# Splitting the float64 weights with a sloped ReLU, with guard, shift and query scaling on VectorE

## The chip, the cores and the metric

The kernel runs on one NeuronCore of a Trainium2 chip. The metric is the device time of one execution in microseconds (us), as the median of several runs. Engine names are those of the profile: PE is TensorE (PEld its weight loads), DVE is VectorE, ACT is ScalarE, POOL is GpSimd, SP is SyncE, which issues most DMAs.

## The reference

Attention with a threshold, then a SwiGLU feed-forward block. The batch is 8, with 8 heads, 576 positions and 64 values a head; the block has 4608 tokens, width 512 and inner width 1536.

```python
scores = scale * np.matmul(q, k.transpose(0, 1, 3, 2))      # scale = 1/8
thresh = np.max(scores, axis=-1, keepdims=True) - tau
scores = np.where(scores >= thresh, scores, -1000000000.0)
attn = np.exp(scores - np.max(scores, axis=-1, keepdims=True))
attn = attn / (np.sum(attn, axis=-1, keepdims=True) + 1e-09)
x = (attn @ v)            # -> (8*576, 512)
...
g = x @ w_gate
silu = g * (1.0 / (1.0 + np.exp(-g)))
return (silu * (x @ w_val)) @ w_out
```

q, k and v are float32. The three weight matrices come as float64.

## The kernel before

**Stages.** The first batch is worked through in two passes, ahead of everything else. Pass one (stage 1, to about 51 us) goes over four pairs of heads with two score tiles of 128 queries each, eight tiles T0 to T7. Pass two (stage 2, to about 129 us) goes over the pairs again with the three tiles that are left of each, the third a half tile (L468); plain products of the feed-forward block (L571) are filled in between. Stage 3 (to about 269 us) brings the first of the later batches, with jobs that a planner puts in order by costs and due times written in the code, and the output products of the first batch. After that a steady state runs to the end, in which PE alternates scores, weighted sums and the products of the feed-forward block. In stages 1 and 2 the order on each engine is the order in which the code issues, tile by tile: the loop over `segs[:2 * NP]` calls `scores`, and between its `next(go)` steps the other work.

**A tile.** PE makes the scores of two heads into two PSUM tiles (L462). DVE takes the maximum of each (L479, two reductions), ACT the exponential (L482, twice) and the threshold (L484), DVE the masks with their sums (L487, twice, which free the PSUM tiles), then the total and its reciprocal (L489, L490). The next tile needs the same PSUM. PE transposes the masked tile (L517, L520), multiplies it by v (L545, L548, L550), ACT copies (L557) and POOL multiplies the two heads' parts (L558). At the end of a tile DVE transposes k and q of the next pair (L682, L685) or the rest of q (L770). The factor 1/8 of the scores is applied to q: by DVE for the first pair (L684), for the others by POOL (L395, queued by `scales`).

**The weights.** [...]

- `split_weights`: ACT reads the upper word as float32 and writes its scaled absolute value (L322); ACT turns the lower word into a small number (L323).
- `clamp` (L315): bounds the absolute value. It runs on POOL in stages 1 and 2, and on DVE for two pieces of stage 3.
- `shift_weights`: DVE shifts the result left by three bits (L342). The exponent field comes out as that of float32.
- `join_weights`: DVE puts the sign back, which it takes from the upper word in the place of the load (L348, between L479 and L487 of the next tile). Then the place is free for the next load.
- `add_lower`: POOL adds the lower word's contribution to the bits (L358).

In stage 3 the last pieces go the same way as jobs: L890 and L893 on ACT, L315, L900 and L902 on DVE, L904 on POOL. In stage 2 three tiles handle two pieces at once (`double`).

**Score order (L462).** Head 0 first, in two halves of 288 keys, then head 1 in pieces of 64, 224 and 288 keys.

**Halves.** The sigmoid is made of a tanh, and several factors of one half are put into ACT's scale operand (the tanh's argument, the copies of the sums) or into a DVE operation (L1083, L1209).

## Time and profile before

| | us |
|---|---|
| median of 3 runs | 1366.19 (1366.06 to 1366.28) |
| profiled execution, its own time | 1368.65 |
| span of the profile of that execution | 1366.5 |
| mean granted clock of PE | 0.996 |

The profile comes from one execution. Its own time is 2.15 us above the span, for what lies around the program, and 2.46 us above the median of the unprofiled runs. A row of the timeline has the start, the duration, the engine, the line and operation, the tile written and the tiles read (partitions x elements), a count, and in brackets the idle time of the engine ahead of it with what ended that. Rows in sequence may overlap by some 0.08 us, since an engine starts the next instruction before the last has left it.

### The profile page before, as it was taken

What the parts mean: (1) busy time and instruction counts of PE and PEld (TensorE: products, weight loads), DVE (VectorE), ACT (ScalarE), POOL (GpSimd) and SP (SyncE); (2) the same over time, 40 slices, a digit from 0 to 9 for tenths busy, and PEclk for the clock granted to TensorE, in tenths of its full rate; (3) what the DMA queues carried; (4) which work ended last, traced back from release to release, by engine and by line L of the source; (5) the groups of instructions that cost most, each with busy time, mean ns of one, the idle gap of its engine ahead of it and who ended that gap; (6) DMA issues with size and microseconds to landing.
All of it is one profiled execution on the core that took longest, in us unless ns stands there. A gap on an engine that the chain in (4) does not pass through costs nothing.

```text
span 1366.5 us, 39110 instructions
## 1 busy us (share of the span) xinstructions
PE 1346.2 (99%) x15598; PEld 1124.6 (82%) x15598; DVE 1094.1 (80%) x2860; ACT 857.4 (63%) x2190; POOL 710.8 (52%) x676
## 2 busy tenths in 40 slices
PE   8899999999999999999999999999999999999998
PEld 6687877777788788877888788888887788999888
DVE  6889898888887878887878777887888776797786
ACT  6788765677765777677767677677767674330330
POOL 2777698754655669434963387337843592000000
PEclk9999999999999999999999999999999999999999
DMA  7753323466426431654255514643255404424411
GB/s 173 192 197 102 72 60 114 129 177 179 114 48 167 149 81 46 183 144 113 45 170 137 152 19 138 158 139 68 74 156 145 110 27 158 149 77 142 160 54 32
DMA packets 208293, 162.31 MB, mean 119 GB/s; under 512 B 166128, under 2 KB 180464, under 8 KB 202736
## 3 DMA queue, kind: packets, MB, share of 16 engines
q1 hardware_dynamic: 203920, 158.86, 41.3%
q8 instruction: 123, 2.02, 0.6%
q10 hardware_dynamic: 4192, 0.95, 0.3%
q14 instruction: 58, 0.48, 0.1%
HBM read 138.28 MB, written 21.50 MB: 117 GB/s over the span
## 4 chain that ended last, share of the span: by engine, by line
PE 91%; DVE 4%; DMA 2%; SPq 1%; ACT 1%; issue 1%; ACTq 0%; DVEq 0%
PE pb L1012 17%; PE pa L1012 12%; PE px L1501 12%; PE sc L1761 10%; PE pe L1012 9%; PE xa L1895 9%; PE po L1294 5%; PE py L1510 5%; PE sc L1179 1%; PE sc L462 1%; PE pe L1179 1%; PE pg L1225 1%; PE pv L571 1%; PE sc L1012 1%; PE pg L571 1%
## 5 line engine op out<-in xcount | busy, mean ns | idle before, releaser
L1837 ACT ACTIVATE pall<-sc,nm 128x288 f32<-128x288 f32 x504 | 234.7, 501 | 79.1 <-DVE pall L1839 43.9
L1839 DVE SCALAR_TENSOR_TENSOR pall<-sc,th,pall 128x288 f32<-128x288 f32 x504 | 243.6, 512 | 38.5 <-ACT pall L1837 22.0
L1012 PE MATMUL pb<-xall,big 128*128 128x256 f32 x1104 | 262.0, 380 | 0.0
L1012 PEld LDWEIGHTS pb<-xall,big 128*128 128x128 f32 x1104 | 207.5, 190 | 29.6 <-issue 1.6
L1874 DVE STREAM_TRANSPOSE pall<-pall 128x576 f32<-128x576 f32 x252 | 187.9, 763 | 28.7 <-POOL pall L1869 15.2
L1872 ACT ACTIVATE pall<-pall,ri 128x288 f32<-128x288 f32 x416 | 190.5, 526 | 22.7 <-DVE ri L1860 21.9
L1012 PE MATMUL pa<-xall,big 128*128 128x256 f32 x752 | 178.9, 381 | 0.3 <-ACT sc L1019 0.3
L1012 PEld LDWEIGHTS pa<-xall,big 128*128 128x128 f32 x752 | 140.7, 190 | 20.9 <-issue 2.5
L863 POOL TENSOR_TENSOR hall<-hall,tmp 128x512 f32<-128x512 f32 x80 | 102.7, 1283 | 104.8 <-DVE hall L1071 64.5
L1761 PE MATMUL sc<-kT,qT 64*32 64x288 f32 (+1 forms) x5376 | 146.9, 345 | 1.5 <-issue 1.2
L1796 DVE TENSOR_REDUCE mx<-sc 128x2 f32<-128x576 f32 x168 | 118.3, 746 | 35.4 <-PE sc L1761 34.5
L1869 POOL TENSOR_SCALAR pall<-pall,ri 128x288 f32<-128x288 f32 x88 | 88.2, 1010 | 105.1 <-DVE ri L1860 75.9
L1761 PEld LDWEIGHTS sc<-kT,qT 64*32 64x32 f32 x5376 | 98.0, 106 | 53.3 <-issue 12.8
L1012 PE MATMUL pe<-xall,big 128*128 128x256 f32 x576 | 138.4, 383 | 0.0
L1895 PE MATMUL xa<-pall,vall 64*32 64x288 f32 x4032 | 129.4, 404 | 3.0 <-PE px L1501 2.7
L1012 PEld LDWEIGHTS pe<-xall,big 128*128 128x128 f32 x576 | 107.6, 190 | 18.7 <-issue 4.5
L1895 PEld LDWEIGHTS xa<-pall,vall 64*32 64x32 f32 x4032 | 83.4, 107 | 41.7 <-issue 5.0
L863 POOL TENSOR_TENSOR tmp<-tmp 128x512 f32<-128x512 f32 x36 | 45.9, 1276 | 83.5 <-ACT tmp L1093 83.5
L1854 ACT COPY sums<-sums 32x6 f32<-32x6 f32 x336 | 66.6, 198 | 28.0 <-DVE pall L1839 23.8
L1070 ACT ACTIVATE vall<-tmp 128x512 f32<-128x512 f32 x96 | 60.0, 627 | 34.5 <-DVE tmp L1083 27.2
L1510 PE MATMUL py<-wo,hall 128*128 128x256 f32 x336 | 74.8, 379 | 0.0
L863 POOL TENSOR_TENSOR hall<-hall 128x384 f32<-128x384 f32 (+2 forms) x67 | 67.6, 1023 | 8.9 <-PE px L1501 8.2
(268 smaller groups left out, 2493.7 us busy)
## 6 DMA issues: line engine op xcount, KB each, us to landing
big<-sums_hbm SPq DMA_DIRECT2D x42, 1024.0 KB, 5.2
big<-sums_hbm SPq DMA_DIRECT2D x48, 768.0 KB, 4.8
vall<-in_v_dram SPq DMA_DIRECT2D x112, 144.0 KB, 3.0
out_dram<-big SPq DMA_DIRECT2D x32, 256.0 KB, 2.9
qT<-in_q_dram SPq DMA_DIRECT2D x112, 72.0 KB, 4.8
kT<-in_k_dram SPq DMA_DIRECT2D x112, 72.0 KB, 3.1
wo<-in_moe_w_gate_dram SPq DMA_DIRECT2D x16, 384.0 KB, 4.2
wo<-in_moe_w_val_dram SPq DMA_DIRECT2D x16, 384.0 KB, 5.1
```

Of the source, the lines that this page charges most:

```text
L863: return lambda: nc.gpsimd.tensor_tensor(out=out, in0=a, in1=b, op=op)
L1012: nc.tensor.matmul(ps[:, i], w[:, k_, i * P:(i + 1) * P], x[:, k_, :], start=first and i == k_ == 0, stop=True, skip_group_check=True)
L1501: nc.tensor.matmul(ps, a[:, f, :], ws[n][:, f, :], start=bank_ not in begun, stop=True, skip_group_check=True)
L1510: nc.tensor.matmul(ps(), a[:, f, i * P:(i + 1) * P], operands[o][:, f, :], start=first and f == 0, stop=True, skip_group_check=True)
L1761: nc.tensor.matmul(to[g * G:(g + 1) * G], qT[hs, col:col + G], kT[hs, c * SH + lo:c * SH + hi], start=True, stop=True)
L1796: rs.append(job("DVE", 0.72 if w > 1 else 0.42, lambda h=h: nc.vector.tensor_reduce(out=mx[:, n0 + h:n1 + h + 1:max(2, n1 - n0), 0], in_=s ...
L1837: ej = job("ACT", 0.44, lambda x=x, n=n: nc.scalar.activation(ps[x], scs[x], AF.Exp, bias=nm[:, n:n + 1]), ej, rank=top, on=on[x])
L1839: masks[x] = job("DVE", 0.48, lambda x=x, n=n: nc.vector.scalar_tensor_tensor(out=ps[x], in0=scs[x], scalar=th[:, n:n + 1], in1=ps[x], op0 ...
L1869: scaled.append(job("POOL", 1.02, lambda x=x, n=n: nc.gpsimd.tensor_scalar(out=x, in0=x, scalar1=ri[:, n:n + 1], scalar2=None, op0=ALU.mul ...
L1872: scaled.append(job("ACT", 0.46, lambda x=x, n=n: nc.scalar.activation(x, x, AF.Copy, scale=ri[:, n:n + 1]), rj, rank=rank))
L1874: seg["turned"].append(job("DVE", 0.72, lambda both=both: nc.vector.transpose(out=both, in_=both), *scaled, rank=rank))
L1895: nc.tensor.matmul(holds[a].ap()[x * G:(x + 1) * G, 0:SH].rearrange("d (i q) -> d i q", q=G), vr[rs, h, j, ds], p[rs, h, :, j, :], start=( ...
```

## The change

- The upper word is read through a sloped ReLU (`Prelu`), so that the sign stays and the xor (L348, L902) is gone; `join_weights`, `clamp_split` and `add_lower` go with it.
- The clamp works on the upper 16 bits of each result as an integer, on DVE, directly ahead of the shift. Both stand at the end of a tile, where the shift stood. POOL's add is issued right behind the shift.
- The lower word becomes an integer by ACT's conversion on output. A place is free for the next load when ACT has read the lower word.
- q of the first batch is scaled by DVE directly ahead of each transpose (128x256 with the pair's k and q, 128x320 for the rest of q).
- The five score products of a tile alternate between the heads: head 0's first half, head 1's 64 and 224, head 0's second half, head 1's second.
- Most factors of one half leave ACT's scale operand and are collected in the copies of the attention's sums (0.5 in the first batch, 0.25 later).

By the order of the instructions on each engine: POOL loses 22 clamps and 7 scalings; DVE loses 24 xors and gains 22 clamps on top of the two that it had and 7 scalings on top of the one; PE has the five products of stage 1's and 2's tiles in another order; SP issues two pieces of weights of stage 1 ahead of a v load and, in stage 3, the last piece ahead of a k and q load. ACT's instructions keep their shapes.

```diff
@@ -309,66 +311,46 @@
     def words(place, dst, w):
         return places[place].bitcast(U32).rearrange("p (m n w) -> p m n w", m=dst.shape[1], w=2)[:, :, :, w]
 
-    early_slots, clamped, unclamped, shifted, unsummed = [True], [], deque(), [], []
 
     def clamp(eng, x):
-        eng.tensor_scalar(out=x, in0=x, scalar1=1.875 * 2.0 ** -80, scalar2=2.0 ** -111, op0=ALU.min, op1=ALU.max)
+        top = x.bitcast(I16).rearrange("p m (n w) -> p m n w", w=2)[:, :, :, 1]
+        eng.tensor_scalar(out=top, in0=top, scalar1=float((32 << 7) - 2 ** 15), scalar2=float((31 << 7) + (7 << 4)), op0=ALU.max, op1=ALU.min)
+
+    def upper(dst, place):
+        nc.scalar.activation(dst, words(place, dst, 1).bitcast(F32), AF.Prelu, scale=2.0 ** -112, alpha=2.0 ** 32)
+
+    def lower(lo, dst, place):
+        nc.scalar.activation(lo.bitcast(I32), words(place, dst, 0), AF.Copy, bias=2.0 ** 23, scale=2.0 ** -29)
 
     def split_weights():
         if fetched:
             dst, place = fetched.popleft()
             lo = los[0].rearrange("p (m n) -> p m n", m=dst.shape[1])
             los.rotate(1)
-            nc.scalar.activation(dst, words(place, dst, 1).bitcast(F32), AF.Abs, scale=2.0 ** -96)
-            nc.scalar.activation(lo, words(place, dst, 0), AF.Identity, bias=minus2, scale=-2.0 ** -51)
-            unclamped.append(dst)
-            if early_slots[0]:
-                clamp_split()
+            upper(dst, place)
+            lower(lo, dst, place)
+            used.discard(place)
             split.append((dst, place, lo))
 
-    def clamp_split():
-        while unclamped:
-            dst = unclamped.popleft()
-            clamp(nc.gpsimd, dst)
-            clamped.append(dst)
+    def shift(dst):
+        ub = dst.bitcast(U32)
+        clamp(nc.vector, dst)
+        nc.vector.tensor_scalar(out=ub, in0=ub, scalar1=3, scalar2=None, op0=ALU.logical_shift_left)
 
     def shift_weights(n=1):
 
-        steps = [split.popleft() for _ in range(min(n, len(split)))]
-        if any(up is x for up, place, lo in steps for x in unclamped):
-            clamp_split()
-        for up, place, lo in steps:
+        for up, place, lo in [split.popleft() for _ in range(min(n, len(split)))]:
             ub = up.bitcast(U32)
-            nc.vector.tensor_scalar(out=ub, in0=ub, scalar1=3, scalar2=None, op0=ALU.logical_shift_left)
-        shifted.extend(steps)
-
-    def join_weights():
-        for up, place, lo in shifted:
-            ub = up.bitcast(U32)
-            nc.vector.scalar_tensor_tensor(out=ub, in0=words(place, up, 1), scalar=0x80000000, in1=ub,
-                                           op0=ALU.bitwise_and, op1=ALU.bitwise_xor)
-            used.discard(place)
-        unsummed.extend(shifted)
-        shifted.clear()
-        add_lower(min(1, len(unsummed)))
-
-    def add_lower(n):
-        for up, place, lo in unsummed[:n]:
-            ub = up.bitcast(U32)
+            shift(up)
             nc.gpsimd.tensor_tensor(out=ub, in0=ub, in1=lo.bitcast(U32), op=ALU.add)
             joined.append(up)
-        del unsummed[:n]
 
     def need(n):
-        if len(joined) < n:
-            join_weights()
-            add_lower(2)
         while len(joined) < n:
             fetch_weights(2)
             if not split:
                 split_weights()
             shift_weights()
-            join_weights()
             split_weights()
 
     raw_places = {0: h1all[:, 0:2 * S], 1: extra[:, 0:2 * S], 2: extra[:, 2 * S:4 * S], 3: h1all[:, 2 * S:4 * S]}
@@ -405,17 +387,12 @@
                 nc.vector.tensor_scalar(out=cap, in0=tau_s, scalar1=0.0, scalar2=2e38, op0=ALU.is_ge, op1=ALU.mult)
                 nc.vector.tensor_scalar(out=cap, in0=cap, scalar1=-1e38, scalar2=None, op0=ALU.add)
                 nc.vector.scalar_tensor_tensor(out=cut, in0=tau_s, scalar=-1.0, in1=cap, op0=ALU.mult, op1=ALU.min)
-            elif i == 1:
-                scale(raws[0][:, 0:QA])
-            else:
-                scales.append(lambda: scale(raws[0][:, 0:QA]))
 
             own = h1all[:, 4 * S:5 * S - QA] if i == 0 else raws[0][:, QA:S]
             raws.append(own)
 
             def load_rest():
                 load("q", slice(QA // G, NJ), [nc.sync] * 2, own.rearrange("p (j d) -> p j d", d=G))
-                scales.append(lambda: scale(own))
 
             more_loads.append(load_rest)
         else:
@@ -444,9 +421,6 @@
 
     heads = [slice(h * D, (h + 1) * D) for h in range(2)]
 
-    def turned(t):
-        return t < NT
-
     def statistics(*names):
         return [stp.tile([P, 2 * MU, 2] if x == "mx" else [P, 2 * MU], F32, name=x) for x in names]
 
@@ -455,12 +429,10 @@
         q0 = t * P - seg["q0"]
         if t < NT:
             pss = [next_sc() for _ in range(2)]
-            for h, hs in enumerate(heads):
-                cut_ = D if turned(t) and h == 1 else 0
-                for n, lo, to in [(0, 0, D), (0, D, SH), (1, 0, SH)] if cut_ else [(0, 0, SH), (1, 0, SH)]:
-                    at_ = (n * SH + lo - cut_) % S
-                    nc.tensor.matmul(pss[h][:, n, lo:to], qT[hs, q0:q0 + P], kT[hs, at_:at_ + to - lo],
-                                     start=True, stop=True)
+            for h, n, lo, to in ((0, 0, 0, SH), (1, 0, 0, D), (1, 0, D, SH), (0, 1, 0, SH), (1, 1, 0, SH)):
+                hs, at_ = heads[h], (n * SH + lo - h * D) % S
+                nc.tensor.matmul(pss[h][:, n, lo:to], qT[hs, q0:q0 + P], kT[hs, at_:at_ + to - lo],
+                                 start=True, stop=True)
         else:
             pss = [next_sc()]
             for n, h in ((0, 0), (1, 1), (1, 0), (0, 1)):
...
@@ -554,7 +526,7 @@
         rbufs.rotate(1)
 
         def weigh():
-            nc.scalar.copy(both, xa[:, 0:2 * n])
+            nc.scalar.activation(both, xa[:, 0:2 * n], AF.Copy, scale=0.5)
             nc.gpsimd.tensor_tensor(out=to, in0=both[:, 0:n], in1=both[:, n:2 * n], op=ALU.mult)
 
         copy(xa, weigh)
...
@@ -669,6 +641,9 @@
         if i < NPAIR and i not in raws and i not in kept:
             raws[i] = load_qk(i)
 
+    def scale_q(x):
+        nc.vector.tensor_scalar(out=x, in0=x, scalar1=scl, scalar2=None, op0=ALU.mult)
+
     def prepare(seg):
         i = seg["i"]
         if i in kept:
@@ -680,8 +655,7 @@
             qT = qkp.tile([P, S], F32, name="qT")
             kT, rest_ = kTs[i], rests[i]
             nc.vector.transpose(out=kT, in_=kr)
-            if i == 0:
-                nc.vector.tensor_scalar(out=qr[:, 0:QA], in0=qr[:, 0:QA], scalar1=scl, scalar2=None, op0=ALU.mult)
+            scale_q(qr[:, 0:QA])
             nc.vector.transpose(out=qT[:, 0:QA], in_=qr[:, 0:QA])
             later.append((rest_, raws[i][2]))
             kept[i] = {"kT": kT, "qT": rest_, "q0": QA}
@@ -714,13 +688,11 @@
     more_loads.popleft()()
     last = iter(())
     for n, seg in enumerate(segs[:2 * NP]):
-        early_slots[0] = n < NP
         if n >= NP:
             seg["v"] = segs[seg["i"]]["v"]
         for x, t in enumerate(seg["tiles"]):
             go = scores(seg, t)
             next(go)
-            join_weights()
             if not n and not x:
                 run_idle(6)
             next(last, None)
@@ -748,8 +720,6 @@
                 split_weights()
                 fetch_weights(2)
             next(go)
-            clamp_split()
-            add_lower(1)
             double = t == NT and NP <= n < NP + 3
             if more and not double:
                 shift_weights()
@@ -759,7 +729,6 @@
             if double:
                 shift_weights(2)
                 split_weights()
-                clamp_split()
                 fetch_weights(2)
             gates()
             last = go
@@ -767,17 +736,14 @@
                 later.rotate(1)
             if later and (n == NP or n == NP - 1 and x == 0):
                 to, fr = later.popleft()
+                scale_q(fr)
                 nc.vector.transpose(out=to, in_=fr)
             if x == 0 and 0 < n < NP - 1:
                 load_v(segs[n + 1])
                 more_loads.popleft()()
-            if n == 0 and x == 1 or n == 1:
-                scales.popleft()()
-            elif n == NP - 2 and x == 1:
+            if n == NP - 2 and x == 1:
                 more_loads.popleft()()
-                scales.popleft()()
             elif n == NP - 1:
-                scales.popleft()()
                 fetch_qk(NP)
             elif n == NP and x == 1:
                 scales.popleft()()
@@ -785,7 +751,6 @@
                 prepare(segs[n + 1])
 
     fill(left[0])
-    join_weights()
     fetch_weights()
     gates()
 
@@ -887,23 +852,17 @@
                 before = joins[-3] if len(joins) > 2 else None
 
                 def up_part(dst=dst, place=place):
-                    nc.scalar.activation(dst, words(place, dst, 1).bitcast(F32), AF.Abs, scale=2.0 ** -96)
+                    upper(dst, place)
 
                 def lo_part(dst=dst, place=place, lo=lo):
-                    nc.scalar.activation(lo, words(place, dst, 0), AF.Identity, bias=minus2, scale=-2.0 ** -51)
+                    lower(lo, dst, place)
 
                 j = job("ACT", 0.93, up_part, j if srcs else landed, done.get(place), under, rank=2)
-                j = job("ACT", 1.03, lo_part, j, before, rank=2)
+                j = done[place] = job("ACT", 1.03, lo_part, j, before, rank=2)
             ub = dst.bitcast(U32)
-            if not any(dst is x for x in clamped):
-                j = job("DVE", 0.6, lambda dst=dst: clamp(nc.vector, dst), j, rank=2)
-            j = job("DVE", 0.6, lambda ub=ub: nc.vector.tensor_scalar(
-                out=ub, in0=ub, scalar1=3, scalar2=None, op0=ALU.logical_shift_left), j, rank=2)
-            j = job("DVE", 0.96, lambda ub=ub, dst=dst, place=place: nc.vector.scalar_tensor_tensor(
-                out=ub, in0=words(place, dst, 1), scalar=0x80000000, in1=ub, op0=ALU.bitwise_and, op1=ALU.bitwise_xor), j, rank=2)
+            j = job("DVE", 1.2, lambda dst=dst: shift(dst), j, rank=2)
             j = job("POOL", 1.85, lambda ub=ub, lo=lo: nc.gpsimd.tensor_tensor(out=ub, in0=ub, in1=lo.bitcast(U32), op=ALU.add), j, rank=2)
             joins.append(j)
-            done[place] = j
         return joins
 
     stores, summed_g, parts = {}, {}, []
...
@@ -1080,8 +1039,7 @@
         def p3(self):
             m = self.mul(self.e, self.w[5], xs[2], False, self.s5, *self.w_deps[5], *ready_x[self.c][4])
             u = self.u1_buf
-            g1 = job("DVE", 0.7, lambda: nc.vector.scalar_tensor_tensor(out=u.ap, in0=self.e.rows(), scalar=0.5, in1=u.ap, op0=ALU.mult,
-                                                                        op1=ALU.add), m, self.u1, rank=0)
+            g1 = job("DVE", 0.7, lambda: nc.vector.tensor_tensor(out=u.ap, in0=self.e.rows(), in1=u.ap, op=ALU.add), m, self.u1, rank=0)
             self.e.read_by(g1)
             self.e.done(True)
             self.finish(0, u, g1, self.a, self.m2)
...
@@ -1903,8 +1861,9 @@
         lo, at_last = 0, 2 * NT * G
         for a in range(R):
             def copy(a=a):
-                nc.scalar.copy(xk[:, a], holds[a].ap()[:, lo:lo + 2 * NT * G].rearrange("p (t i q) -> p t i q", t=2, q=G))
-                nc.scalar.copy(xl[:, a], holds[a].ap()[:, at_last:at_last + G])
+                nc.scalar.activation(xk[:, a], holds[a].ap()[:, lo:lo + 2 * NT * G].rearrange("p (t i q) -> p t i q", t=2, q=G),
+                                     AF.Copy, scale=0.25)
+                nc.scalar.activation(xl[:, a], holds[a].ap()[:, at_last:at_last + G], AF.Copy, scale=0.25)
             js.append(job("ACT", 0.65, copy, m, last_store[0] if cc == 0 else None, rank=0))
             holds[a].read_by(js[-1])
             holds[a].done(False)
```

## The prediction, made before the changed kernel was run

> **What bounds the kernel now.** I read the page first, then the windows by stage, the waits of PE, and the timelines of DVE, POOL and PE around the longest wait.
>
> ```profile
> PE 1346.2 (99%) x15598; PEld 1124.6 (82%) x15598; DVE 1094.1 (80%) x2860; ACT 857.4 (63%) x2190; POOL 710.8 (52%) x676
> ```
>
> PE is busy for 99% of the span, so a change pays only where PE waits or runs slowly. The windows show where that is.
>
> ```profile
> core 0: us, PE busy (x) PEld busy (x) DVE busy (x) ACT busy (x) POOL busy (x), PEclk, DMA share, GB/s
> 0.00:51.25 51.25, 42.44 (x299) 33.77 (x300) 38.59 (x91) 33.18 (x63) 23.82 (x28) 0.90 0.82 191
> 51.25:128.93 77.68, 76.15 (x609) 60.01 (x610) 66.32 (x127) 63.46 (x120) 56.49 (x50) 1.00 0.49 152
> 150.00:182.00 32.00, 31.57 (x435) 26.33 (x433) 31.36 (x85) 22.47 (x64) 25.79 (x24) 1.00 0.19 39
> 269.00:1366.00 1097.00, 1088.76 (x12814) 921.00 (x12798) 863.87 (x2289) 666.79 (x1752) 520.21 (x498) 1.00 0.41 116
> ```
>
> Stage 1 (to 51.25, eight score tiles T0 to T7) leaves PE idle for 8.8 us, at a mean granted clock of 0.90. Stage 2 leaves 1.5. From 150 to 182 DVE is busy 98% of the time, PE idle 0.4. Nothing that matters changes after 269.
>
> ```profile
> PE sc L462 <- DVE pall L487: 6.3, 5, 3.7
> ```
>
> A score tile cannot start before the masks (L487) of the tile before have freed its PSUM: five waits, 6.3 us, the longest 3.7. That one is the stall below, first on DVE, then on POOL, then on PE.
>
> ```profile
> 32.19 0.17 DVE L490 RECIPROCAL ri<-tot 128x2 f32<-128x2 f32 x1
> 34.79 0.88 DVE L342 TENSOR_SCALAR big<-big 128x768 uint32<-128x768 uint32 x1 [2.43 <-POOL big L315]
> 36.61 1.38 DVE L479 TENSOR_REDUCE nm<-sc 128x1 f32<-128x576 f32 x2
> 37.92 1.05 DVE L348 SCALAR_TENSOR_TENSOR big<-wo,big 128x768 uint32<-128x768 uint32 x1
> 40.76 1.10 DVE L342 TENSOR_SCALAR big<-big 128x768 uint32<-128x768 uint32 x1
> ```
>
> ```profile
> 30.83 0.93 POOL L395 TENSOR_SCALAR hall<-hall,scl 128x256 f32<-128x256 f32 x1 [5.97 <-DMA hall<-in_q_dram]
> 31.72 1.81 POOL L358 TENSOR_TENSOR big<-big,extra 128x768 uint32<-128x768 uint32 x1
> 33.92 0.83 POOL L315 TENSOR_SCALAR big<-big 128x768 f32<-128x768 f32 x1
> 39.63 1.81 POOL L358 TENSOR_TENSOR big<-big 128x768 uint32<-128x768 uint32 x1
> ```
>
> ```profile
> 39.76 3.24 PE L462 MATMUL sc<-pall,qT 64*128 64x288 f32 x10 [3.74 <-DVE pall L487]
> ```
>
> POOL's queue stands behind a q scaling that waits for its load, so the clamp is late, the shift waits 2.43 behind the clamp, and T6 starts after 3.74 of idle PE. The granted clock then is 0.50 from 38.96 to 45.79: T6 takes 3.24, where tiles at full clock take 1.36 to 2.09.
>
> Also to be seen: the shift at 40.76 takes 1.10 and ends 0.42 after POOL's add of 39.63. Alone it takes 0.54 (row at 46.44). A second case:
>
> ```profile
> 81.39 1.82 POOL L358 TENSOR_TENSOR big<-big,extra 128x768 uint32<-128x768 uint32 x1
> 81.99 2.04 DVE L348 SCALAR_TENSOR_TENSOR big<-wo,big 128x768 uint32<-128x768 uint32 x1
> ```
>
> The xor, 0.95 alone, takes 2.04 and ends 0.82 after the add. DVE's shift or xor and POOL's add do not overlap: the later one waits.
>
> **Stage 1, part by part.** Removed: the clamps L315 and the scalings L395 of the first batch from POOL (0.83 to 1.25 each here), the xors from DVE. Added on DVE: a 16-bit clamp before each shift, a q scaling before each q transpose. No row shows that clamp. Below it lie float clamp and shift of the same 128 x 768 (0.55, 0.54), above it the xor (0.95); I take 0.54, the row that also reads one source. The scaling is 0.31 for 128x256 (L684), about 0.35 for 128x320. ACT's two passes stay two of 128 x 768 (L322 0.93, L323 1.05). The sloped form is in no row; between those two I price it at 0, since ACT is idle by 0.49 and 0.50 around its early pieces, and a tenth more would hide there.
>
> The xor lay between L479 and L487, mostly beside ACT's exp: L479 to L487 takes 2.21 with it (23.67 to 25.88) and 1.76 without it (two tiles before 17). So a tile loses 0.45 and gains a clamp of 0.54 that nothing hides.
>
> - T1: one scaling, +0.34.
> - End of T2 (from 21.7): clamp 0.54; POOL's product L558 is due and goes first (0.46); shift 0.54, k transpose 0.7. POOL's add starts 0.08 behind the shift and runs 1.82, so the scaling, due 0.7 behind the shift, waits some 1.2 for it; then 0.31 and the q transpose 0.4. L479 of T3 starts near 25.8 against 23.67, +2.1; without the xor T4's scores are 1.65 late.
> - T3 to T5: +1.7. At the end of T4 the 2.43 of waiting is gone, but product, clamp and add come in turn again: from 33.6, 0.54 + 0.46 + 0.54 + 0.08 + 1.82 + 0.31 + 0.4 give L479 near 37.8, against 36.61. T6's scores come at 40.5, +0.8.
> - The half clock costs 2.8 (T6 3.24 for 1.36, its sums 1.92 for 1.04). PE's idle time before T6 would be 2.8 instead of 3.74, so I let half stay: -1.4.
>
> Stage 1 ends near 50.6 instead of 51.25: **-0.6**. Bounds: +0.8 if all of the half clock stays; -2.0 if all goes; -3.8 if the scalings also do not wait for the adds (2.5 of stall and 2.8 of clock, less three scalings and six times 0.09).
>
> The Trainium skill, page "SBUF — State Buffer", section "Who interferes with whom", calls the port pair of VectorE and GpSimd an exclusive lock for a whole instruction. The rows above agree (0.42 and 0.82 past the add's end). By a shared port instead of a lock the sum would take the -3.8.
>
> Score order: in the trace head 1's first product starts 13 ns after head 0's first, though two of head 0 stand ahead of it. Where head 1 waits for the second mask it starts 0.74 later in either order, and head 0's second half then stands behind it. I price it at 0, bounds 0 to +0.15 a waiting tile. The Trainium skill, "TensorE: Matmul & The Clock Gate", Part 2, says that matmuls stay in program order; this trace differs by those 13 ns.
>
> Weight places now come free behind ACT's lower read, so SP issues two pieces ahead of a v load: those pieces land some 4 us earlier (40.76 before), v of the next pair about 40.7, still before T6's sums. If v came later than those sums, PE would wait for the difference; I take 0.
>
> **Stage 2.** Three places (73.2, 91.9, 110.6) handle two pieces in a row: clamp, shift, clamp, shift. POOL's add of the first piece is pending when the second clamp ends, and the second shift follows with 0.03 between. I take it that the pending add goes first. At 73.2: 0.54 + 0.62 + 0.08 + 0.54 + 1.82 + 0.55, then scaling and transpose 0.74; less what overlaps, L479 is near 77.6 instead of 74.80. Without the two xors (2.12) L487 is 1.2 later than at 78.15, and the scores at 79.01 with it. The two others have no scaling: +0.5 and +0.6. What follows regains nothing, since PE is full there (98%). Sum **+2.3**. If DVE keeps the port: L487 comes earlier, and what can be gained is 0.37 of idle PE at 116.31 and 0.73 a tile where head 1 waits (2.09 against 1.36), some -1.7 in all.
>
> **Stage 3.** Six pieces lose xors of 0.95 to 1.36 on DVE and a float clamp; two clamps are there before and shifts stay. PE idle from 128.9 to 214 is 1.25, of which 0.58 waits for ACT. I take the rest: **-0.7**, bounds 0 and -1.25.
>
> **Steady state.** Copy and activation forms cost ACT 580 to 596 ns alike, the half-scaled add 0.69 as the plain one: 0.
>
> **Sum:** -0.6 + 2.3 - 0.7 = +1.0. The profiled execution took 1368.65 (span 1366.5 and 2.15 around it), so 1369.65 for it; the median is 2.46 lower, which gives **1367.2**.
>
> **Rivals.**
> - *Slower: the 16-bit clamp costs what the xor did, 0.95.* For it: its step of two and its type occur nowhere in the trace. Against it: one-source rows of the same size take 0.54. Six tile ends of stage 1 and three first clamps of stage 2 get 0.41 longer (the second clamps lie beside the add), +3.7, in all +4.7: **1370.9**. From 0.75 on it decides.
> - *DVE keeps the port at the double pieces.* -0.6 - 1.7 - 0.7 = -3.0: **1363.2**. For it: DVE issues its next instruction before the last has ended (starts overlap by 0.08 in the rows). Against it: the add asks first.
> - *No wait behind adds at all, for scaling or second shift.* -3.8 - 1.7 - 0.7 = -6.2: **1360.0**. For it: a POOL scaling beside DVE slows it little (0.55 to 0.56 beside L1869). Against it: the two pairs of rows above.
> - *Alternation pays:* if products really start in order, head 1 would start some 0.6 earlier in each of the eight tiles of stage 1, which gives about -5, less what the masks still hold back: **1362**. Against it: 13 ns. (The rule beside it is that of Part 2 of the TensorE page of the Trainium skill.)
>
> **Chances.** Forecast 0.37, slow clamp 0.25, DVE keeps the port 0.19, no waits 0.13, alternation 0.06. The bound of 0.2% (2.73 us, about what a measurement of this kernel can tell from no change) lies at 1363.46 and 1368.92. Faster: 0.01 + 0.17 + 0.13 + 0.05 = 0.36. Slower: 0.06 of the forecast (half clock stays) and 0.24 of the slow clamp, 0.30. Within: 0.34. The forecast's own range is 1365 to 1369.5; with the other cases it is 1360.5 to 1371.2, which leaves out about half of "no waits" and a tenth above.
>
> **What would show it.** Right: the wait of 2.43 gone; scaling rows of about 1.5 behind the k transpose at the ends of T2 and T4; T3's L479 near 25.8; scores of T6 near 40.5 after 2 to 3 of idle PE; second shifts of 2.4 at the three doubles; clamp rows of 0.54; from 269 on the same distance to the end. Wrong: scalings of 0.31 there, clamp rows of 0.95, T6 at full clock, PE waiting for v.

## The result, and the profile after

The changed kernel takes 1374.44 us (median of 7 runs, 1370.40 to 1375.52) against 1366.53 for the kernel before (7 runs). The ratio is 1.0044, with a 95% interval of 1.0030 to 1.0058: slower by some 6 us (the two medians lie 7.9 apart). The profiled execution took 1374.44, its span is 1372.5, 6.0 more than the span before. One execution, of e6_before_filled in the table of the experiments, took 2314.55 us at a mean clock of 0.556 and is left out of its ratio.

The page of the changed kernel, first the engines:

```profile
PE 1350.1 (98%) x15598; PEld 1123.8 (82%) x15598; DVE 1088.4 (79%) x2865; ACT 854.4 (62%) x2190; POOL 678.0 (49%) x647
```

DVE and POOL both have less to do than before (1088 for 1094, 678 for 711), and the kernel is slower. The sum of the work is not the reason. The windows by stage, with the same bounds as before:

```profile
core 0: us, PE busy (x) PEld busy (x) DVE busy (x) ACT busy (x) POOL busy (x), PEclk, DMA share, GB/s
0.00:51.25 51.25, 43.84 (x288) 33.24 (x288) 39.63 (x92) 31.12 (x59) 12.61 (x17) 0.87 0.87 208
51.25:128.93 77.68, 73.35 (x575) 56.80 (x571) 57.52 (x124) 59.02 (x115) 36.34 (x30) 0.98 0.47 141
...
150.00:182.00 32.00, 31.46 (x435) 26.29 (x434) 28.48 (x77) 23.41 (x68) 29.45 (x29) 1.00 0.16 29
...
269.00:1372.00 1103.00, 1094.67 (x12959) 923.32 (x12957) 868.81 (x2308) 669.62 (x1763) 520.45 (x498) 1.00 0.41 116
```

The mean granted clock of the first window fell from 0.90 to 0.87, and of the second from 1.00 to 0.98. DVE is busy 1.0 us more than before in the first and 8.8 us less in the second. The last window is 6 longer and holds 6 more of PE's work only because the same work comes 6 later; from stage 3's first scores to the end it takes as long as before (worked out below). PE's waits:

```profile
PE sc L434 <- DVE pall L459: 8.5, 7, 2.5
```

Seven waits of score tiles for the masks, 8.5 us, where there were five of 6.3. The longest is 2.5 instead of 3.7. Line numbers have moved: L434 is L462 of before, L459 is L487, L451 is L479, L338 the shift, L317 the new clamp, L645 the q scaling, L345 POOL's add. On DVE, the ends of T2 and T4 and the second double (a double handles two pieces of 128 x 768 weights in a row):

```profile
23.49 0.77 DVE L338 TENSOR_SCALAR big<-big 128x768 uint32<-128x768 uint32 x1
24.18 0.77 DVE L657 STREAM_TRANSPOSE pall<-extra 128x576 f32<-128x576 f32 x1
24.88 1.43 DVE L645 TENSOR_SCALAR extra<-extra,scl 128x256 f32<-128x256 f32 x1
...
26.72 1.38 DVE L451 TENSOR_REDUCE nm<-sc 128x1 f32<-128x576 f32 x2
...
35.12 0.60 DVE L317 TENSOR_SCALAR big<-big 128x768 int16<-128x768 int16 x1
35.76 0.56 DVE L338 TENSOR_SCALAR big<-big 128x768 uint32<-128x768 uint32 x1
...
36.93 1.44 DVE L645 TENSOR_SCALAR hall<-hall,scl 128x256 f32<-128x256 f32 x1
...
38.78 1.38 DVE L451 TENSOR_REDUCE nm<-sc 128x1 f32<-128x576 f32 x2
...
96.22 0.63 DVE L317 TENSOR_SCALAR big<-big 128x768 int16<-128x768 int16 x1
96.88 2.01 DVE L338 TENSOR_SCALAR big<-big 128x768 uint32<-128x768 uint32 x1
```

POOL's adds at the same places:

```profile
24.34 1.82 POOL L345 TENSOR_TENSOR big<-big,extra 128x768 uint32<-128x768 uint32 x1 [0.49 <-DVE big L338]
...
36.41 1.82 POOL L345 TENSOR_TENSOR big<-big 128x768 uint32<-128x768 uint32 x1 [1.75 <-DVE big L338]
...
96.38 2.08 POOL L345 TENSOR_TENSOR big<-big,extra 128x768 uint32<-128x768 uint32 x1 [3.64 <-DVE big L338]
99.03 1.80 POOL L345 TENSOR_TENSOR big<-big 128x768 uint32<-128x768 uint32 x1 [0.56 <-DVE big L338]
```

The add starts at 24.34 and runs to 26.16; the scaling of 24.88 ends at 26.31, 0.15 behind it, and takes 1.43 instead of 0.31. The same happens at 36.41 and 36.93. At 96.38 the add starts beside the second clamp and takes 2.08 instead of 1.82; the second shift of 96.88 ends 0.43 behind the add and takes 2.01. Read as in the prediction, the pending add goes as soon as the clamp has ended, and the shift waits for it. The clamp by itself takes 0.60.

The score tiles that wait, and the stretches of half clock:

```profile
16.59 3.24 PE L434 MATMUL sc<-pall,qT 64*128 64x288 f32 x10 [1.91 <-DVE pall L459]
...
24.47 1.36 PE L434 MATMUL sc<-pall,qT 64*128 64x288 f32 x10
...
41.41 3.23 PE L434 MATMUL sc<-pall,qT 64*128 64x288 f32 x10 [2.54 <-DVE pall L459]
...
82.20 2.09 PE L434 MATMUL sc<-pall 64*128 64x288 f32 x10 [1.38 <-DVE pall L459]
...
120.73 2.09 PE L434 MATMUL sc<-pall 64*128 64x288 f32 x10 [1.01 <-DVE pall L459]
```

```profile
core 0: us, PE busy (x), PEclk, DMA share, GB/s
17.30:24.13 6.83, 6.83 (x38) 0.50 0.93 260
41.20:48.03 6.83, 6.62 (x35) 0.50 0.97 282
123.10:126.50 3.40, 3.40 (x28) 0.50 0.02 5
```

The third column of the last fence is the granted clock. The half clock lasts 6.83 us from 17.3, 6.83 from 41.2 and 3.41 from 123.1, 17.1 us in all. Before it was 3.41 from 18.5 and 6.83 from 39.0, 10.2 in all.

Where the 6.0 come in, by the starts of the score tiles against those of before:

| place | late by | what came in |
|---|---|---|
| T2 (16.59) | 0.48 | the scaling ahead of T1, and 0.09 at the start |
| T3 (24.47) | 2.07 | T2 to T3 7.88 instead of 6.29: two windows of half clock instead of one |
| T4 (29.35) | 2.60 | the scaling behind the add |
| T6 (41.41) | 1.65 | the wait of 2.43 is gone, the second scaling waits |
| end of stage 1 (53.05) | 1.80 | T6 at half clock as before |
| behind the doubles | 3.19, 3.79, 4.42 | the second shifts: 1.38, 0.60, 0.63 |
| last half tile (129.03) | 6.02 | 8.30 instead of 6.70 from tile to tile: the half clock at 123 |
| end | 6.0 | stage 3 adds 0.6, and 0.6 is regained behind it |

So 2.6 come from the doubles, 3.5 from half clock (1.59 from T2 to T3; 0.29 from T6 to T7, which takes 7.43 instead of 7.14; 1.60 at 123), and the queues of stage 1 by themselves give -0.1. This is read from two executions, one of each kernel; e4 below bears on it.

### The profile page after: what moved, and what is told of

Its sections match the earlier page's. It is cut to its first block, busy times and chain, and to the rows that moved or that the text cites. A ratio compares the mean times of both kernels' runs of the same rounds, so it can differ in the third digit from the quotient of the medians.

```text
span 1372.5 us, 39057 instructions
## 1 busy us (share of the span) xinstructions
PE 1350.1 (98%) x15598; PEld 1123.8 (82%) x15598; DVE 1088.4 (79%) x2865; ACT 854.4 (62%) x2190; POOL 678.0 (49%) x647
## 4 chain that ended last, share of the span: by engine, by line
PE 91%; DVE 5%; ACT 2%; issue 1%; DMA 1%; POOL 0%; SPq 0%; DVEq 0%; ACTq 0%; POOLq 0%
PE pb L971 17%; PE pa L971 12%; PE px L1459 12%; PE sc L1719 10%; PE pe L971 9%; PE xa L1853 9%; PE py L1468 5%; PE po L1252 4%; PE sc L434 1%; PE pg L1183 1%; PE sc L1137 1%; PE pv L1183 1%; PE pe L1137 1%; PE pv L543 1%; PE sc L971 1%
## 5 line engine op out<-in xcount | busy, mean ns | idle before, releaser
L1797 DVE SCALAR_TENSOR_TENSOR pall<-sc,th,pall 128x288 f32<-128x288 f32 x504 | 243.8, 513 | 39.9 <-ACT pall L1795 23.6
```

Of the source, the lines that this page charges most:

```text
L1797: masks[x] = job("DVE", 0.48, lambda x=x, n=n: nc.vector.scalar_tensor_tensor(out=ps[x], in0=scs[x], scalar=th[:, n:n + 1], in1=ps[x], op0 ...
```

## The experiments

Two theories. "Lock": DVE's scaling and second shift wait for POOL's add, since the shift now releases the add directly ahead of them. "Clock": the idle time that this makes on PE brings more stretches of half clock, and those are the larger part. Its opposite in the expectations, "chain", says that only the waits for VectorE count. The rivals are in the expectations. Each kernel was timed against the kernel before on the same chip.

| kernel | median, us | ratio to before | 95% interval |
|---|---|---|---|
| the changed kernel | 1374.44 | 1.0044 | 1.0030 to 1.0058 |
| e1_fill | 1375.26 | 1.0052 | 1.0039 to 1.0065 |
| e2_scale_first | 1369.63 | 1.0014 | 1.0005 to 1.0023 |
| e3_doubles | 1369.65 | 1.0011 | 1.0001 to 1.0022 |
| e4_order | 1372.54 | 1.0038 | 1.0025 to 1.0052 |
| e5_fill_transposes | 1373.73 | 1.0044 | 1.0032 to 1.0057 |
| e6_before_filled | 1369.46 | 1.0013 | 1.0004 to 1.0022 |
| e7_before_scale_vector | 1368.54 | 1.0007 | 0.9998 to 1.0016 |
| e8_after_scale_gpsimd | 1368.95 | 1.0003 | 0.9994 to 1.0012 |
| c1_both | 1363.45 | 0.9973 | 0.9963 to 0.9984 |
| c2_both_filled | 1364.76 | 0.9981 | 0.9972 to 0.9990 |
| c3_both_order | 1362.80 | 0.9968 | 0.9956 to 0.9981 |
| c4_pair1_gpsimd | 1363.51 | 0.9968 | 0.9956 to 0.9980 |

### e2: the scaling ahead of the shift

```diff
-            scale_q(qr[:, 0:QA])
+            if i == 0:
+                scale_q(qr[:, 0:QA])
...
+            if n + 1 < NP and x == len(seg["tiles"]) - 2:
+                scale_q(raws[n + 1][0][:, 0:QA])
             if more and not double:
                 shift_weights()
```

> The changed kernel with one order changed on VectorE: at the ends of T2 and T4 the q scaling stands ahead of the clamp and shift instead of behind the k transpose. Lock theory: the scaling then takes 0.31 instead of 1.43, since GpSimd's add is released only by the shift behind it; T3's first reduction comes some 0.9 earlier, T5's some 2 earlier, stage 1 ends 1 to 2 us earlier, and 1 to 2 us come off the time if the half-clock windows stay where they are. Rival (the scaling is slow by itself, or the transposes take the add's time instead): the scaling row stays above 1 us or the k transpose grows, and nothing is gained.

DVE at the end of T4:

```profile
32.88 0.35 DVE L645 TENSOR_SCALAR hall<-hall,scl 128x256 f32<-128x256 f32 x1
33.15 0.60 DVE L317 TENSOR_SCALAR big<-big 128x768 int16<-128x768 int16 x1
33.78 0.56 DVE L338 TENSOR_SCALAR big<-big 128x768 uint32<-128x768 uint32 x1
34.26 0.77 DVE L657 STREAM_TRANSPOSE pall<-hall 128x576 f32<-128x576 f32 x1
34.95 0.41 DVE L660 STREAM_TRANSPOSE qT<-hall 128x256 f32<-128x256 f32 x1
35.28 1.39 DVE L451 TENSOR_REDUCE nm<-sc 128x1 f32<-128x576 f32 x2
```

The scaling takes 0.35, and neither shift nor transposes grow, although POOL's add runs beside the transposes. T5's first reduction comes at 35.28 instead of 38.78. Stage 1 ends at 48.52 instead of 53.05, more than expected, for this execution had only 3.4 us of half clock in stage 1 (from 39.9; another 3.4 from 118.0). The ratio falls by 0.30 points, some 4 us, where 1 to 2 were expected; by its trace, part of that is clock. The lock theory holds here. The Trainium skill, "SBUF — State Buffer", section "Who interferes with whom", says that, where a VectorE instruction in a 2-port mode meets GpSimd, whoever issues first gets the shared ports for the whole instruction; 1.43 behind the add and 0.35 ahead of it agree. Whether these rows run in such a mode no run here shows.

### e3: clamp, clamp, shift, shift

```diff
-        for up, place, lo in [split.popleft() for _ in range(min(n, len(split)))]:
-            ub = up.bitcast(U32)
-            shift(up)
+        steps = [split.popleft() for _ in range(min(n, len(split)))]
+        for up, place, lo in steps:
+            clamp(nc.vector, up)
+        for up, place, lo in steps:
+            ub = up.bitcast(U32)
+            nc.vector.tensor_scalar(out=ub, in0=ub, scalar1=3, scalar2=None, op0=ALU.logical_shift_left)
             nc.gpsimd.tensor_tensor(out=ub, in0=ub, in1=lo.bitcast(U32), op=ALU.add)
```

> The changed kernel with the two pieces of a double handled as clamp, clamp, shift, shift instead of clamp, shift, clamp, shift, so that GpSimd's first add is released only when the second shift is next. Lock theory: the second shift falls from some 2.4 to 0.6 us, the score tiles behind the doubles lose their idle 1.4, 0.6 and 1.0, stage 2 is 2.6 us shorter, and with the idle the half clock near 123 goes too, another 1.6: 1370 to 1372. Rival (the added clamps are the cost, not the lock): the starts behind the doubles move by under 0.5 each and the time by under 1.5.

DVE at the first double (the scaling) and at the second (clamps and shifts):

```profile
75.57 1.96 DVE L648 TENSOR_SCALAR extra<-extra,scl 128x320 f32<-128x320 f32 x1
...
93.53 1.11 DVE L317 TENSOR_SCALAR big<-big 128x768 int16<-128x768 int16 x2
94.52 1.02 DVE L347 TENSOR_SCALAR big<-big 128x768 uint32<-128x768 uint32 x2
```

PE's score tiles behind the three doubles:

```profile
80.63 2.09 PE L437 MATMUL sc<-pall 64*128 64x288 f32 x10 [1.18 <-DVE pall L462]
...
99.25 1.36 PE L437 MATMUL sc<-pall 64*128 64x288 f32 x10
...
116.71 1.38 PE L437 MATMUL sc<-pall 64*128 64x288 f32 x10
```

Two shifts take 1.02 together. Behind the second and third double the tile starts with no idle time and takes 1.36 to 1.38 instead of 2.09, since both masks are done. At the first double the wait has only moved to the scaling, which stands behind the first shift there: 1.96, and 1.18 of idle PE. From the tile ahead of the first double (72.95) to the last half tile (122.70) it is 49.75 instead of 54.72 in the changed kernel, 5.0 less: 0.2, 0.6 and 1.0 at the three starts, the waits of head 1, and the half clock at 123, which is gone. The ratio falls by 0.33 points, 4.5 us; the median of 1369.65 lies just below the 1370 to 1372 expected.

### e4: the score order of before

```diff
-            for h, n, lo, to in ((0, 0, 0, SH), (1, 0, 0, D), (1, 0, D, SH), (0, 1, 0, SH), (1, 1, 0, SH)):
+            for h, n, lo, to in ((0, 0, 0, SH), (0, 1, 0, SH), (1, 0, 0, D), (1, 0, D, SH), (1, 1, 0, SH)):
```

> The changed kernel with the score products in the order of before: head 0 whole, then head 1. Forecast: alternation is worth nothing, so the time stays within 1 us of the changed kernel and a score tile takes 1.36 (both PSUM tiles free) or 2.09 (head 1 waits). Rival 'alternation costs': head 0's second half stands behind head 1's wait, 0.15 a waiting tile, and this kernel is up to 1 us faster. Rival 'alternation pays': this kernel is 1 us or more slower.

Score tiles take 1.36 and 2.09, as in the changed kernel. The median is 1.9 lower, but the intervals overlap over most of their length, and the profiled execution had 6.8 us of half clock instead of 17.1. It can't be told from nothing here; see c3.

This trace also tests the reading of the half clock above. But for the score order its queues are those of the changed kernel, and it has one stretch at T2 (from 18.5), one at T6 (from 42.4) and none behind the doubles:

```profile
16.47 2.09 PE L434 MATMUL sc<-pall,qT 64*128 64x288 f32 x10 [1.91 <-DVE pall L459]
22.73 1.36 PE L434 MATMUL sc<-pall,qT 64*128 64x288 f32 x10
...
118.31 2.09 PE L434 MATMUL sc<-pall 64*128 64x288 f32 x10 [0.99 <-DVE pall L459]
125.01 1.19 PE L440 MATMUL sc<-pall 64*64 64x288 f32 x8
```

T2 to T3 takes 6.26, as before the change (6.29) and not 7.88; from the third double's tile to the half tile it is 6.70, as before and not 8.30. So the delays of 1.59 and 1.60 come and go with the stretches, at the same idle time ahead of them. Stage 3's scores start at 130.94 instead of 134.95: 4.0 us for 10.2 us less of half clock, 0.39 for each.

### e1, e5, e6: filling PE's idle time

```diff
+            fillers = {(1, 0): 4, (2, 0): 2, (3, 0): 5, (5, 1): 3, (6, 1): 1, (7, 1): 2}.get((n, x), 0)
+            if fillers:
+                run_idle(fillers)
             go = scores(seg, t)
```

> The changed kernel with matmuls that nothing reads (128x256, as at the start of the kernel) put ahead of six score tiles, as many as fit into PE's idle time there: 4 before T2, 2 before T4, 5 before T6 (1.9, 0.9 and 2.5 us idle), and 3, 1 and 2 before the tiles that wait behind the double pieces. Theory 'clock': most of what the forecast missed is that PE's idle gaps bring half-clock windows (17.1 us of them in the profile of after, 10.2 in that of before). Then T2 and T6 run at full clock, T3 starts some 2 to 3 us earlier than 24.5, T7 some 2 earlier than 48.8, the window at 123 goes, and the time falls by 4 to 7.5 us to 1367 to 1370. Theory 'chain': the waits for VectorE set the pace and the clock only fills time that would be idle anyway; then the score tiles keep their starts within 0.5 us and the time stays within 1 us of 1374.

T2 ran at full clock, and T3 started at 21.31 instead of 24.47, as "clock" says. But the filling matmuls wait themselves, for a PSUM bank that ACT has yet to copy:

```profile
28.28 1.13 PE L267 MATMUL idle<-pall 128*128 128x256 f32 x4 [2.58 <-ACT pall L529]
```

This held back T4 to 29.34, T6 to 44.63 and stage 1 to 54.15. The median of 1375.26 fits neither theory ("clock" expected 1367 to 1370, "chain" at most 1 us from 1374). As a test of the whole it failed. In the next two, transposes are repeated in their own place:

```diff
-                    nc.tensor.transpose(end[:, 0:P], both, ident)
+                    for _ in range(1 + {(0, 0): 15, (1, 0): 9, (2, 0): 20}.get((seg["i"], t), 0)):
+                        nc.tensor.transpose(end[:, 0:P], both, ident)
```

> A cleaner filling than e1, whose added matmuls waited for ACT to free a PSUM bank. The changed kernel with the last 128x128 transpose of three tiles repeated into its own PSUM place: 15 times ahead of T2, 9 ahead of T4, 20 ahead of T6, at some 0.11 us each, inside PE's idle time there. Theory 'clock': the granted clock stays at 1.00 to the end of stage 1, T2 to T3 takes 4.7 instead of 7.9, T6 to T7 some 5 to 6 instead of 7.4, stage 1 ends between 48.5 and 50.6 instead of 53.1, and the median falls by 3 to 5 us to some 1370, with less scatter between runs; what is left over the kernel before is about 2. Theory 'chain': score starts from T4 on stay within 0.5 us of the changed kernel's.

Stage 1 of the profiled execution ends at 50.34 instead of 53.05, but a half-clock stretch came at 29.7 and another of 6.8 us at 80.9, behind the idle time of the first double, so the profiled time is 1374.01. The five runs are at 1371.58 to 1374.50: the two with mean clocks of 0.998 and 1.000 took 1371.58 and 1371.71, the three at 0.996 took 1373.73 to 1374.50. Even at 1.000 the kernel is some 4 us above the kernel before. The median is 0.7 under the changed kernel's, not the 3 to 5 expected.

> The kernel before with the same repeated transposes in its two long idle times: 12 ahead of T2 (1.5 us idle) and 30 ahead of T6 (3.7 idle). Theory 'clock': the half-clock windows of 18.5 and 39.0 go, T6 takes 2.1 or less instead of 3.2, and the median falls by 2 to 3.5 us. The distance from this kernel to e5 is then what VectorE's and GpSimd's queues alone make of the change, some 2 to 4 us. Theory 'chain': no change beyond 1 us.

The kernel before has no half clock left in it: T6 starts at 38.64 without idle time and takes 1.36.

```profile
38.64 1.36 PE L462 MATMUL sc<-pall,qT 64*128 64x288 f32 x10
```

Stage 3's scores start at 125.65 instead of 128.93. So 10.2 us of half clock cost 3.3 us there, 0.32 for each, and the 6.8 more of the changed kernel should cost 2.2 at that rate; by the starts of its tiles it was 3.5. Yet the median is 2 above the kernel before, where 2 to 3.5 below were expected. From stage 3 to the end the profiled execution is 1.2 longer, with the same instructions; a row of PE's waits from 300 on shows where.

```profile
PE sc L1762 <- issue: 1.7, 3, 0.6
```

"Issue" stands for time in which PE waits for nothing that the profile shows. Before, this wait is there once (1.2). Here it is there three times, near 340, 636 and 1077, and at each the distance to the kernel before grows by 1.0 to 1.1; the one of before, near 783, costs 1.6. The kernels with added PE instructions (e1, e5, e6, c2) have such stalls near 636 and 1077, three of them also near 340; those without have one near 780 (e4 one more). So the added instructions move the stalls. What they are is open. Nor do they explain the whole median: the profiled execution of e6 took 1366.54, the shortest of its runs and 2.1 less than the profiled one of before, and what the others lose, at clocks of 0.999 to 1.000, is in no trace. So the timed medians of e1, e5, e6 and c2 carry microseconds that are not of the question, and mainly the starts up to 130 us are used.

### e7 and e8: the scaling by itself, and the rest by itself

e7 is the kernel before with the first batch's q scaled by VectorE; e8 is the changed kernel with it scaled by GpSimd. The main lines of e7 (GpSimd's scalings are taken out as well):

```diff
             nc.vector.transpose(out=kT, in_=kr)
-            if i == 0:
+            if True:
                 nc.vector.tensor_scalar(out=qr[:, 0:QA], in0=qr[:, 0:QA], scalar1=scl, scalar2=None, op0=ALU.mult)
             nc.vector.transpose(out=qT[:, 0:QA], in_=qr[:, 0:QA])
...
+                nc.vector.tensor_scalar(out=fr, in0=fr, scalar1=scl, scalar2=None, op0=ALU.mult)
                 nc.vector.transpose(out=to, in_=fr)
```

> One part of the change alone: the kernel before with q of the first batch scaled by VectorE instead of GpSimd, all else (weights, score order) as before. In it GpSimd's add is released only by the xor of the next tile, so no add is pending when the scaling comes. Lock theory: scaling rows of 0.31 to 0.40 everywhere, the 2.43 of waiting at 32 us gone, T6 2 us earlier, and 1363 to 1365.5, clearly below the kernel before: the part is good and only its place behind the released add spoils it. Rival (the scaling itself is too much for VectorE): level with before or slower.

PE at T2 and behind the first double:

```profile
16.52 3.23 PE L457 MATMUL sc<-pall,qT 64*128 64x288 f32 x10 [1.91 <-DVE pall L482]
...
78.99 2.09 PE L457 MATMUL sc<-pall 64*128 64x288 f32 x10 [1.04 <-DVE pall L482]
```

Level with before: the expected gain of 2.5 to 5 isn't there. The wait of 2.43 is gone and T6 has 1.6 of idle time ahead of it instead of 3.7. But T2 starts 0.41 later with 1.91 idle, and T2 to T3 took 7.86 with two windows of half clock; and behind the first double 1.04 of idle time is new, where the shifts take 1.60 together and the scaling 0.94, beside POOL's clamps. Stage 3 starts at 128.93, exactly where it did.

> The other side of it: the changed kernel with q of the first batch scaled by GpSimd as before. Lock theory: the k and q transposes of the ends of T2 and T4 lose the waiting scaling (1.4 each), stage 1 ends 1.5 to 3 us earlier than in the changed kernel, while the doubles of stage 2 stay 0.5 to 1.2 us late each: 1369.5 to 1371.5, like e2. Rival (scaling on VectorE is a gain also here): level with the changed kernel or slower, as GpSimd's queue would again wait for a load.

The median is 5.5 under that of the changed kernel and level with before, a little below the 1369.5 to 1371.5 expected. Stage 1 ends at 48.51, 4.5 earlier where 1.5 to 3 were expected (half clock is 3.4 us in this execution); the doubles keep 0.97, 0.55 and 0.99 of idle time. GpSimd's queue does wait for a load again, its add is late for that, and the clamp on DVE ends 0.47 behind the add:

```profile
30.11 0.93 POOL L377 TENSOR_SCALAR hall<-hall,scl 128x256 f32<-128x256 f32 x1 [5.35 <-DMA hall<-in_q_dram]
...
31.42 1.82 POOL L345 TENSOR_TENSOR big<-big 128x768 uint32<-128x768 uint32 x1
...
32.17 1.54 DVE L317 TENSOR_SCALAR big<-big 128x768 int16<-128x768 int16 x1
```

So the scaling on VectorE costs 0.6 us in the old weight path, which is inside the interval of e7 and may be nothing, and 5.5 in the new one, with the half clock that comes with it. It is the pair of edits that is slow: in the old path the xor of the next tile released the add, after the scaling; in the new one the shift releases it, ahead of the scaling. For the ends of T2 and T4 e2 shows this by itself.

### c1 to c4: the orders put right

c1 has the edits of e2 and e3, and the scaling of the first double ahead of its clamps:

```diff
             if double:
+                if n == NP and later:
+                    scale_q(later[0][1])
                 shift_weights(2)
...
-                scale_q(fr)
+                if not double:
+                    scale_q(fr)
                 nc.vector.transpose(out=to, in_=fr)
```

> The changed kernel with the orders of e2 and e3 together, and the q scaling of the first double piece moved ahead of its clamps as well, since in e3 it took 1.96 behind the first shift. Lock theory: no VectorE row waits for a GpSimd add any more at these places; each of the three score tiles behind the doubles starts with less than 0.3 idle, stage 1 is 1.5 to 4.5 us shorter than in the changed kernel, stage 2 some 3 to 4.5 shorter, and the median is 1364.5 to 1367, level with the kernel before or up to 2 us below it. Rival (gains do not add, since PE is full behind): no better than 1369, as e2 or e3 alone.

DVE at the first double, and PE's tiles behind the three doubles:

```profile
70.78 0.38 DVE L648 TENSOR_SCALAR extra<-extra,scl 128x320 f32<-128x320 f32 x1
71.07 1.11 DVE L317 TENSOR_SCALAR big<-big 128x768 int16<-128x768 int16 x2
72.05 1.04 DVE L347 TENSOR_SCALAR big<-big 128x768 uint32<-128x768 uint32 x2
```

```profile
76.50 1.65 PE L437 MATMUL sc<-pall 64*128 64x288 f32 x10
...
94.69 1.36 PE L437 MATMUL sc<-pall 64*128 64x288 f32 x10
...
112.15 1.37 PE L437 MATMUL sc<-pall 64*128 64x288 f32 x10
```

No operation waits for an add there, no tile waits for the masks, and the tiles take 1.36 to 1.65. The ratio is 0.9973, 3.7 us under the kernel before. The changed kernel is 0.71 points or some 10 us away (11 by the medians). The gains of e2 and e3, 0.30 and 0.33, add, and the scaling of the first double comes on top; the median lies 1 us below the range expected. Stage 2 takes 75.24 us (48.81 to 124.05) instead of 81.90. The seven runs lie within 1.9 us of each other, with mean clocks of 0.997 to 0.999; those of the changed kernel lie within 5.1, at 0.992 to 0.997.

> c1 with 14, 10 and 10 repeated transposes ahead of T2, T4 and T6 (idle 1.8, 1.4, 1.4 there in e2). If the clock is a cost of its own, another 1 to 2.5 us below c1 and the fastest of all, 1363 to 1365, with little scatter. If the windows seldom fall in c1, no difference.

Clock 1.000 in the profiled execution, stage 3 starts 0.7 earlier than in c1, and yet the median is 1.3 above c1, against what was expected. In the profiled execution the stalls for "issue" do it (1.87 at 336.69, 0.57 and 0.46 later, against one of 0.36 in c1). The intervals of the two kernels overlap.

> c1 with the score products in the order of before. In e4 the order's effect was inside the scatter. If alternation costs or gains nothing, the median is that of c1 within 0.7 us, at some 1363.5; if it gains, this is 1 us or more above c1, if it costs, 1 or more below.

0.65 under c1, inside the bound of 0.7 that was set for "nothing". The two comparisons of the order, e4 and c3, point the same way, and neither is outside its interval. What alternation costs, if anything, stays open below about 2 us.

> c3 with one scaling given back: q of the second pair, the one ahead of T1, is scaled by GpSimd, which is idle then. It isolates the one scaling that no add disturbs: 0.31 on VectorE ahead of T1's reduction, which makes T2 start 0.2 to 0.5 later and PE's idle time ahead of T2 1.8 instead of 1.5. Theory 'clock': the shorter idle time makes half-clock windows at T2 rarer, and the median falls by 0.3 to 1.5 below c3's 1362.8, with T2 at 16.1. Theory 'chain': 0.3 and no more, 1362.5.

T2 starts at 16.25 with 1.52 idle, and the profiled execution had a half-clock window from 17.7 all the same; that of c3, with 1.79 idle, had none there. The ratio is that of c3. So in these two executions 0.3 us less of idle time at T2 did not decide whether a window falls there; the "clock" expectation of 0.3 to 1.5 was not met.

## Why the prediction was wrong, step by step

The forecast was 1367.2 and level; the measured time is above its range (to 1371.2), on the slower side. In the span 5.0 us were missed (+1.0 forecast, +6.0 measured), and the points below account for these. In the median 7.2 were missed: the last step of the sum took off the 2.46 by which the profiled execution before lay above its median, and the profiled execution of the changed kernel is itself the median. With 21 to 23 runs the median of the kernel before is 1367.3 to 1368.0, so of the 2.46 only 0.7 to 1.3 would be left with more runs.

- **Lock, right.** It was the forecast's main mechanism. Scalings at the ends of T2 and T4: near 1.5 forecast, 1.43 and 1.44 measured. Doubles: 1.2, 0.5 and 0.6 forecast, 1.38, 0.60 and 0.63 measured. The second shifts take 2.01 where 2.4 was forecast. The pending add goes first, as taken. e2, e3 and c1 show it by removing it. The price of the rival "DVE keeps the port" was too small: its own terms, 0.37 and three times 0.73, make 2.6 and not 1.7, and c1's stage 2 is 2.4 shorter than that of the kernel before.
- **Clamp, right.** 0.54 taken, 0.60 measured. The rival with 0.95 is out, although its number, 1370.9, is the nearest to the result: that is luck.
- **The wait of 2.43, right.** It is gone, and T6 still came late, with 2.54 of idle time (2.8 forecast).
- **Half clock, the step that failed.** The sum said that half of its 2.8 at T6 would stay, "-1.4". It stayed whole at T6, it doubled at T2, and a new stretch came at 123: +3.5 instead of -1.4, which is 4.9 of the 5 us missed in the span. Its worst bound for stage 1, +0.8, was that all of the half clock stays; that there could be more of it stood in no bound, and stage 1 came out at +1.80. The forecast looked for half clock only where the profile of before had it longest. It had made T2 0.34 later and put waits of 0.5 to 1.2 behind the doubles, and never asked which clock the next tile would then run at. A single profile was also read as if the stretches had a fixed place. Their starts differ from trace to trace (16.3 to 18.5 near T2), and so do the times: 1370.40 at a mean clock of 0.997, 1375.52 at 0.992. The profiled pair is still a typical one: the seven runs of the changed kernel have a mean clock of 0.994 on average, those of the kernel before 0.996 to 0.997 in each round of experiments.
- **Stage 1's queues, mis-sized.** +0.8 without the clock was forecast, -0.1 measured. Part of the waits may lie under PE's half clock; no run shows it.
- **Stage 3, wrong.** -0.7 forecast. From its first score tile to the end it takes 1237.55 (134.95 to 1372.5) against 1237.57 before. DVE has less to do (28.48 for 31.36 between 150 and 182), but PE's idle time there did not fall with it: two waits of 0.52 and 0.63 stand where 0.16 and 0.35 were, and both end with DVE's masks. Why these come late was not tried.
- **Alternation, copies and factors.** Nothing measurable, as forecast. The rival that had alternation gain 5 is out by e4 and c3. Copies and factors had no run of their own; that stage 3 to the end takes as long as before is all that speaks for them. No wait of PE for a load of v shows.

The Trainium skill, "TensorE: Matmul & The Clock Gate", Part 1, tells of a free-running window of 3413 ns that sets the clock. The lengths of 3.41 and 6.83 and the changing starts agree. That page of the Trainium skill speaks of a whole idle window as the cause; here 1.0 us of idle time ahead of 120.73 was followed by half clock from 123.1, which is less than it asks for, and the measurement decides. But the idle time alone does not settle it: the same 1.0 us stands ahead of the third double's tile in five traces, and a stretch followed in two of them (the changed kernel and e2) and not in e4, e5 and e8.

How much of the 6 us is clock stays a range. By the starts of the tiles in one profile it is 3.5; for the 6.8 us more of half clock it is 2.7 by the rate of e4 and 2.2 by that of e6. The step of the forecast was thus off by 3.6 to 4.9 (-1.4 instead of +2.2 to +3.5). The fillings meant to settle it moved other stalls.

## What to carry to other kernels

When an operation is moved to an engine that waits out whole operations of another, as VectorE does here with GpSimd's adds, ask which instruction releases the other engine's next long operation, and put everything short that would wait ahead of that instruction. Two edits that are each level can be slow together for that reason, and changes of order alone were worth some 10 us here. Idle time on PE can have a second price, the clock of the next microseconds: a forecast that adds waits of one microsecond has to give each of them a chance of half clock behind it, here at 0.3 to 0.5 us lost for each microsecond of it.

## What the runs showed that was not expected

- Repeated matmuls in idle time took away the half clock (0.996 to 1.000 in e6) and made stage 3 start 3.3 us earlier, and by the median the kernel was 2 us slower all the same. PE stalls for "issue" at three later places instead of one, which is 1.2 us in the profiled execution; the rest is open.
- One microsecond of idle PE was followed by a stretch of 3.4 us at half clock in two of five traces.
- The time of the changed kernel goes with how much of such stretches an execution gets: the same program was at 1370.40 with a mean clock of 0.997 and at 1375.52 with 0.992.
